# Squared-ReLU attention with a gated convolution network on one core: v's loads of batch 0 moved behind the planes' transfers, four banks for block 0's scores, and all low parts of the gated values on GpSimd

## The chip, the cores and the metric

The kernel runs on one core of one Trainium2 chip. The metric is the device time of one execution in microseconds (us), lower is better; the median of several runs is shown, and one further execution was taken with the hardware profiler. The engines are named as in the profile: PE (TensorE matmul; PEld its weight loads), DVE (VectorE), ACT (ScalarE), POOL (GpSimd), SP (SyncE, which here issues nearly all DMAs).

## The reference, cut to what matters

```python
# u, v: (4, 3136, 256), z: (4, 3136, 64)
scores = (1.0 / S) * np.matmul(z, z.transpose(0, 2, 1))      # S = 3136
attn = np.maximum(scores, 0.0) ** 2
x = u * np.matmul(attn, v)                                   # (4, 3136, 256)

h = np.maximum(x @ w_in, 0.0)                                # d_ff = 1024
conv_out[s] = sum(conv_w[k] * h_padded[s + k] for k in (0, 1, 2))   # per channel
gate = 1.0 / (1.0 + np.exp(-conv_out))
out = h * gate @ w_out                                       # (4, 3136, 256)
```

## The kernel before, in words

**Number format.** Most products are made from two 32-bit parts of each operand: a rounded "high" part (`ah`, `vh`, `gh`, `xh`, `zhh`) and the rest, "low" = value minus high (`al`, `vl`, `gl`, `xl`, `zll`). A product is three matmuls: high by low, high by high, low by high. Every value that goes into a matmul therefore costs one copy (`copy`, at line 125 of the profile for some) and one subtraction (`sub`, line 122 of the profile whoever runs it, on DVE or on POOL).

**Blocks and slots.** The 3136 rows of a batch are cut into 7 blocks of 448 columns (`QB = 7`), 28 blocks in all; q is the block's place in its batch. A block goes over the 25 tiles of 128 rows of its batch (`NJ = 25`). One tile of one block is a *slot*, numbered k = 25 * block + place, 700 in all. In slot k PE does the attention product of tile k (`attend`, lines 337 to 342: six matmuls) and then the scores of tile k + 4 (`scores`, lines 253 and 254: two matmuls into a PSUM bank with the tag `s`, of which there are two).

**From scores to attention.** For a computed tile: ACT takes the ReLU (`relu`, tile `t`, 3 buffers), DVE multiplies (`square`), ACT makes `ah`, DVE makes `al` (`split_lo`), which is the last reader of the scores' bank. The scores are symmetric, so later blocks of a batch don't compute every tile again: POOL takes the ReLU'd tile `t` apart into two 16-bit planes (`part`, tile `pl`, 3 buffers, line 270), SP writes them to DRAM (`spill`, `dq<-pl`, line 282), and a later block reads them back transposed (`fetch`, `tp<-dq`, line 290), joined by POOL (`join`, `tj<-tp`, line 296). Block q takes 0, 3, 7, 10, 14, 17 and 21 of its 25 tiles this way for q = 0 to 6. Block 0 of the kernel transposes nothing and spills most.

**v.** Two tiles of v at a time are loaded by SP (`load_v`, tile `vst`, 3 buffers, line 168), copied to `vh` by ACT (DVE for the first) and split to `vl` by POOL (`prep_v`). For batch 0 this runs inside block 0: tile j is prepared in slot j - 3.

**The network.** While block b + 1 does its attention, the network of block b runs in eight pieces f of 128 channels, begun in the slots `FS` = 2, 5, 8, 11, 15, 18, 21, 24 of block b + 1. With s the slot of a piece: `ffn_in` in slot s (six matmuls into one of two PSUM banks with the tag `ph`, lines 370 to 372); ReLU to `hb` on ACT and the first tap of the convolution back into the same bank in s + 1; POOL keeps two columns for the next block (`halo`, line 395), waiting for that ReLU; the other two taps on DVE (line 407) in s + 2; the sigmoid on ACT in s + 3; the gate product on DVE (line 421) in s + 4; the high part `gh` on ACT in s + 5; the low part `gl`; and `ffn_out` (lines 438 to 440) from slot s + 10 on.

In the blocks where `(blk + 1) % 7` is 3 to 6 ("V blocks" from here on, named by the block in whose slots the work runs: q = 3, 4, 5, 6) the gate product is written back in place into the `ph` bank, and the low part is made from that bank by DVE in slot s + 6. In the others ("G blocks", q = 0, 1, 2) the gate product goes to an SBUF tile `c`, and POOL makes the low part in slot s + 5. After the last slot, the last block's network runs alone (`last_block`), the tail.

**What sets the order.** Nothing is scheduled: every step is put in a list of its slot by `at(slot, class, ...)`, and the main loop empties the lists in the order of the classes PRE, MID, VEC, POST, PE0, PE1 around the fixed steps. Each engine, SP among them, runs its own instructions strictly in that order, and an instruction that waits holds up all behind it on its engine. Within a slot the POST class comes ahead of `fetch`, `join`, `part` and `spill`; PE1 comes after them, last of all.

Of the kernel before, what the change touches and what calls it, by code (L numbers as in the profile page):

```python
# [8 lines left out]
F32 = mybir.dt.float32  # L9
# [19 lines left out]
LA, LT, LS = 4, 3, 2  # L29
# [1 line left out]


FS = [2, 5, 8, 11, 15, 18, 21, 24]
RELU, TAP, ST1, ST2, SIG, GATE, GHI, GLO, OUT0, OUT1 = 1, 1, 2, 2, 3, 4, 5, 6, 10, 11
EVAC = 12
XS = 1

C_GATE, C_ST1, C_ST2, C_G, C_SIG, C_HI, C_LO = 0, 2, 2, 2, 3, 3, 2
C_TAP, C_XS, C_EV, C_V = 3, 3, 3, 5

QV = 3


WS = [0, 8, 11, 17, 15, 21, 27, 22, 29, 34, 36, 38, 40, 45, 48, 53]
# [14 lines left out]
def kernel(  # L59
# [15 lines left out]
    P = 128  # L75
    NB = 448
    QB = S // NB
    NJ = (S + P - 1) // P
# [11 lines left out]
    ps = ctx.enter_context(tc.tile_pool(name="ps", bufs=1, space=bass.MemoryType.PSUM))  # L90
# [14 lines left out]
    def at_slot(k):  # L105
        blk, i = divmod(k, NJ)
        return blk, *ent[blk % QB][i]
# [139 lines left out]
    def scores(k):  # L247
        blk, j, tr = at_slot(k)
        if tr:
            return  # L250
        s = ps.tile([P, 512], F32, tag="s", name="s", bufs=2)
        w = slice(j * P, (j + 1) * P)
        nc.tensor.matmul(s[:, :NB], lhsT=zhh[:, w], rhs=zq[blk], start=True, stop=False)  # L253
        nc.tensor.matmul(s[:, :NB], lhsT=zll[:, w], rhs=zq[blk], start=False, stop=True)  # L254
        sc[k] = s
# [108 lines left out]
    ph, hb, cc, gg, po = {}, {}, {}, {}, {}  # L364
# [30 lines left out]
            nc.gpsimd.tensor_copy(halo[:, f], t[:, NB : NB + 2])  # L395

    def ffn_tap(blk, f):
        e = width(blk)  # L400
        cc[blk, f] = c = ph.pop((blk, f))[:, :e]
        nc.scalar.mul(c, hb[blk, f][:, :e], cw[:, f, 0:1])  # L402
# [68 lines left out]
    V, A, G = nc.vector, nc.scalar, nc.gpsimd  # L471
# [4 lines left out]
    PRE, MID, VEC, POST, PE0, PE1 = range(6)  # L476

    def at(slot, cls, fn, *args):
        ev[slot][cls].append((fn, args))


    for q in range(2, QB):
        s = (7 * q) // 2 - LA - 2
# [1 line left out]
        at(s, POST, prep_z, q)  # L485
    at(-3, POST, prep_z, 1)
    for j in range(2, NJ, 2):
        at(max(j - 9, -LA), POST, load_v, 0, j)
        at(j - 3, C_V, prep_v, j, A)


    for b in range(1, B):
        k0 = (b * QB - 1) * NJ
        for q in range(QB):
            s = k0 - (QB - 2 - q) * NJ + (12 if q % 2 == 0 else 4)
            if q == QB - 2:
                s = k0 + 6
            elif q == QB - 1:
                s = k0 + NJ + 6
            at(s - 4, POST, load_z, b, q)  # L500
            at(s, POST, prep_z, q)
        last = {j: i for i, (j, _) in enumerate(ent[QB - 1])}
        for j in range(0, NJ, 2):
            s = k0 + max(last[j] + 2, last.get(j + 1, 0) + 2, V0 + V1 * j // NJ)
            at(s - 6, POST, load_v, b, j)
            at(s, C_V, prep_v, j, A)
    for blk in range(1, NBLK):
        at(blk * NJ - LA - 2, VEC, queries, blk)
# [2 lines left out]
    for i, (_, what, f) in enumerate(sorted(need)):  # L511
        s = WS[i]
# [8 lines left out]
    for blk in range(NBLK - 1):  # L521
        k0 = (blk + 1) * NJ
        at(k0, C_GATE, gate_x, blk, G)
        at(k0 + XS, C_XS, split_x, blk, (G, G))
        for f in range(FC):
            s = k0 + FS[f]
            at(s, POST, ffn_halo, blk, f)
            at(s, PE1, ffn_in, blk, f)
            at(s + RELU, C_TAP, ffn_relu, blk, f)
            at(s + TAP, C_TAP, ffn_tap, blk, f)  # L530
            at(s + ST1, C_ST1, ffn_conv, blk, f, 1)
            at(s + ST2, C_ST2, ffn_conv, blk, f, 2)
            at(s + SIG, C_SIG, ffn_sig, blk, f)
            lo = V if (blk + 1) % QB >= QV else G
            at(s + GATE, C_G, ffn_gate, blk, f, lo)
            at(s + GHI, C_HI, ffn_hi, blk, f, A)
            at(s + (GLO if lo is V else GHI), C_LO if lo is V else PE1, ffn_lo, blk, f, lo)
            at(s + OUT0, PE0, ffn_out, blk, f, 0)
            at(s + OUT1, PE0, ffn_out, blk, f, 1)
        at(s + EVAC, C_EV, evac, blk)  # L540
        at(s + EVAC + 2, POST, store, blk)
# [28 lines left out]
    with tc.manual_schedule():  # L570
# [12 lines left out]
        for k in range(-LA, max(ev) + 1):  # L583
            e = ev[k]
            run(e[PRE])
            if 0 <= k + LS < NS:
                split_hi(k + LS)
                split_lo(k + LS)
            run(e[MID])
            if 0 <= k + LT < NS:  # L590
                relu(k + LT)
                square(k + LT)
            run(e[VEC])
            run(e[POST])
            if 0 <= k + LD < NS:
                fetch(k + LD)
            if 0 <= k + LJ < NS:
                join(k + LJ)
            if 0 <= k + LP < NS:
                part(k + LP)  # L600
            if 0 <= k + LX < NS:
                spill(k + LX)
            run(e[PE0])
            if 0 <= k < NS:
                attend(k)
            if k + LA < NS:
                scores(k + LA)
            run(e[PE1])
# [41 lines left out]
```

## Time and profile before

| | us |
|---|---|
| median of 3 runs (1699.38 to 1700.0) | 1699.93 |
| the profiled execution | 1699.81 |
| its span, first to last instruction | 1697.7 |
| PE busy in the span | 1615.3 (95%) |
| ACT busy | 1277.1 (75%) |
| DVE busy | 1215.1 (72%) |
| POOL busy | 982.5 (58%) |

The mean granted TensorE clock was 0.992. How to read the views: busy time is the union of an engine's instructions. A matmul of 448 columns is listed at about 367 ns although a new one starts about every 203 ns, because they overlap; so the number of matmuls in a stretch says more about PE than its busy time. The view of waits gives, for each engine and line, who ended its idle time: the total in us, the number of waits, the longest. In the table of stretches each engine's busy us is followed by its number of instructions in brackets.

### The profile page before, as it was taken

What the parts mean: (1) busy time and instruction counts of PE and PEld (TensorE: products, weight loads), DVE (VectorE), ACT (ScalarE), POOL (GpSimd) and SP (SyncE); (2) the same over time, 40 slices, a digit from 0 to 9 for tenths busy, and PEclk for the clock granted to TensorE, in tenths of its full rate; (3) what the DMA queues carried; (4) which work ended last, traced back from release to release, by engine and by line L of the source; (5) the groups of instructions that cost most, each with busy time, mean ns of one, the idle gap of its engine ahead of it and who ended that gap; (6) DMA issues with size and microseconds to landing.
All of it is one profiled execution on the core that took longest, in us unless ns stands there. A gap on an engine that the chain in (4) does not pass through costs nothing.

```text
span 1697.7 us, 24837 instructions
## 1 busy us (share of the span) xinstructions
PE 1615.3 (95%) x7656; PEld 1433.9 (84%) x7656; DVE 1215.1 (72%) x2080; ACT 1277.1 (75%) x2562; POOL 982.5 (58%) x1345
## 2 busy tenths in 40 slices
PE   6689999999999999999999999999999999999998
PEld 5578888888889888888888988889889898888886
DVE  5788667776777767677767766777677776677766
ACT  5577777778777777777887777777877777777785
POOL 5767555556566654546575665555657566445551
PEclk9899999999999999999999999999999999999999
DMA  5543444456324434445543343454634334444540
GB/s 154 154 116 103 111 108 90 106 119 148 107 88 125 109 87 123 99 108 112 124 140 84 107 120 98 102 108 106 133 100 139 93 92 107 103 104 98 109 93 22
DMA packets 384485, 184.59 MB, mean 109 GB/s; under 512 B 275296, under 2 KB 383328, under 8 KB 384352
## 3 DMA queue, kind: packets, MB, share of 16 engines
q1 hardware_dynamic: 384208, 182.77, 43.5%
q8 instruction: 60, 0.98, 0.2%
q14 instruction: 73, 0.60, 0.1%
q10 hardware_dynamic: 144, 0.23, 0.0%
HBM read 36.59 MB, written 80.28 MB: 69 GB/s over the span
## 4 chain that ended last, share of the span: by engine, by line
PE 72%; DVE 13%; issue 6%; ACT 6%; POOL 1%; DMA 1%; SPq 0%; POOLq 0%; DVEq 0%; ACTq 0%
PE av L337 11%; PE av L338 11%; PE av L339 11%; PE ph L370 6%; PE ph L372 5%; PE ph L371 5%; PE s L253 5%; PE o L440 4%; PE o L438 4%; PE o L439 4%; PE s L254 4%; DVE al L122 3%; DVE s L309 3%; DVE ph L407 3%; ACT t L304 2%
## 5 line engine op out<-in xcount | busy, mean ns | idle before, releaser
L122 DVE TENSOR_TENSOR al<-s,ah 128x448 fp32r<-128x448 f32 x672 | 418.1, 622 | 369.1 <-ACT ah L316 198.4
L337 PE MATMUL av<-ah,vl 128*128 128x448 f32 x1344 | 496.0, 369 | 10.2 <-POOL vl L122 7.8
L338 PE MATMUL av<-ah,vh 128*128 128x448 f32 x1344 | 494.6, 368 | 0.0
L339 PE MATMUL av<-al,vh 128*128 128x448 f32 x1344 | 493.1, 367 | 0.0
L296 POOL COPY tj<-tp 128x896 uint16<-128x896 uint16 x288 | 348.4, 1214 | 1.9 <-DMA tp<-dq 1.5
L304 ACT ACTIVATE t<-s 128x448 f32<-128x448 f32 x412 | 225.4, 547 | 129.9 <-PE s L254 104.7
L407 DVE SCALAR_TENSOR_TENSOR ph<-hb,cw,ph 128x448 f32<-128x448 f32 (+1 forms) x448 | 306.8, 685 | 13.1 <-ACT ph L402 5.4
L309 DVE TENSOR_TENSOR s<-s,t 128x448 f32<-128x448 f32 x412 | 258.7, 628 | 78.2 <-ACT t L304 77.2
L270 POOL COPY pl<-t 128x896 uint16<-128x896 uint16 x312 | 290.7, 940 | 14.8 <-DMA dq<-pl 13.8
L395 POOL COPY halo<-hb 128x2 f32<-128x2 f32 x192 | 37.0, 192 | 451.1 <-ACT hb L393 450.7
L316 ACT CAST ah<-s 128x448 fp32r<-128x448 f32 x412 | 219.2, 532 | 98.0 <-DVE s L309 97.0
L337 PEld LDWEIGHTS av<-ah,vl 128*128 128x128 f32 x1344 | 254.6, 189 | 36.4 <-POOL vl L122 10.4
L339 PEld LDWEIGHTS av<-al,vh 128*128 128x128 f32 x1344 | 254.4, 189 | 21.3
L338 PEld LDWEIGHTS av<-ah,vh 128*128 128x128 f32 x1344 | 254.8, 190 | 20.4
L393 ACT ACTIVATE hb<-ph 128x448 f32<-128x448 f32 x224 | 122.6, 547 | 118.8 <-PE ph L372 117.2
L253 PE MATMUL s<-zq,zhh 128*128 128x448 f32 x412 | 163.6, 397 | 39.8 <-DVE al L122 31.0
L370 PE MATMUL ph<-xh,wih 128*128 128x448 f32 x448 | 171.9, 384 | 28.1 <-DVE gl L122 26.0
L314 ACT ACTIVATE ah<-tj 128x448 fp32r<-128x448 f32 x288 | 165.1, 573 | 0.0
L372 PE MATMUL ph<-xl,wih 128*128 128x448 f32 x448 | 164.8, 368 | 0.0
L438 PE MATMUL o<-gh,wol 128*128 128x448 f32 (+1 forms) x448 | 164.7, 368 | 0.0
L440 PE MATMUL o<-gl,woh 128*128 128x448 f32 (+1 forms) x448 | 164.1, 366 | 0.6 <-POOL gl L122 0.6
L371 PE MATMUL ph<-xh,wil 128*128 128x448 f32 x448 | 164.5, 367 | 0.0
(79 smaller groups left out, 2418.3 us busy)
## 6 DMA issues: line engine op xcount, KB each, us to landing
dq<-pl SPq DMA_DIRECT2D x252, 224.0 KB, 2.3
ut<-in_u_dram SPq DMA_DIRECT2D x28, 448.0 KB, 4.1
vst<-in_v_dram SPq DMA_DIRECT2D x48, 256.0 KB, 2.9
dq<-pl SPq DMA_DIRECT2D x84, 112.0 KB, 2.4
out_dram<-ob SPq DMA_DIRECT2D x20, 448.0 KB, 3.3
zt<-in_z_dram SPq DMA_DIRECT2D x28, 224.0 KB, 3.2
tp<-dq SPq DMA_TRANSPOSE x288, 3.3
wr<-in_moe_w_in_dram SPq DMA_DIRECT2D x8, 256.0 KB, 3.6
```

Of the source, the lines that this page charges most:

```text
L122: eng.tensor_tensor(out=out, in0=a, in1=b.bitcast(F32), op=ALU.subtract)
L270: nc.gpsimd.tensor_copy(pl[k], rl.pop(k).bitcast(U16).rearrange("p (n h) -> p h n", h=2))
L296: nc.gpsimd.tensor_copy(tj[k].bitcast(U16).rearrange("p (n h) -> p h n", h=2), t)
L304: nc.scalar.activation(rl[k], sc[k][:, :NB], AF.Relu, scale=SC1)
L309: nc.vector.tensor_tensor(out=s, in0=s, in1=rl[k], op=ALU.mult)
L337: nc.tensor.matmul(o, lhsT=vl[:, j, d], rhs=h, start=first, stop=False)
L338: nc.tensor.matmul(o, lhsT=vh[:, j, d], rhs=h, start=False, stop=False)
L339: nc.tensor.matmul(o, lhsT=vh[:, j, d], rhs=l, start=False, stop=False)
L370: nc.tensor.matmul(o, lhsT=wih[:, dc, w], rhs=xh[blk][:, dc], start=(dc == 0), stop=False)
L371: nc.tensor.matmul(o, lhsT=wil[:, dc, w], rhs=xh[blk][:, dc], start=False, stop=False)
L372: nc.tensor.matmul(o, lhsT=wih[:, dc, w], rhs=xl[blk][:, dc], start=False, stop=(dc == DC - 1))
L407: nc.vector.scalar_tensor_tensor(out=c, in0=hb[blk, f][:, k : e + k], scalar=cw[:, f, k : k + 1], in1=c, op0=ALU.mult, op1=ALU.add,)
```

## The change

Four edits. (1) `load_v` of batch 0 moves from class POST of slot j - 9 to class PE1 of slot j - 7, so behind that slot's `spill`. (2) `load_v` of the later batches moves from POST, six slots ahead of `prep_v`, to PE1, five slots ahead. (3) In block 0 (k < 25) the scores of odd k go to the two `ph` banks, those of even k stay in the two `s` banks. (4) The rule `QV` goes: in every block but the last the gate product goes to the SBUF tile `c`, and POOL makes the low part in class PE1 of slot s + 5. 128 gate products and 128 low parts (16 blocks of 8) are concerned.

```diff
-RELU, TAP, ST1, ST2, SIG, GATE, GHI, GLO, OUT0, OUT1 = 1, 1, 2, 2, 3, 4, 5, 6, 10, 11
+RELU, TAP, ST1, ST2, SIG, GATE, GHI, OUT0, OUT1 = 1, 1, 2, 2, 3, 4, 5, 10, 11
...
-QV = 3
...
-        s = ps.tile([P, 512], F32, tag="s", name="s", bufs=2)
+
+        tag = "ph" if k < NJ and k % 2 else "s"
+        s = ps.tile([P, 512], F32, tag=tag, name="s", bufs=2)
...
     for j in range(2, NJ, 2):
-        at(max(j - 9, -LA), POST, load_v, 0, j)
+        at(max(j - 7, -LA), PE1, load_v, 0, j)
         at(j - 3, C_V, prep_v, j, A)
...
-            at(s - 6, POST, load_v, b, j)
+            at(s - 5, PE1, load_v, b, j)
             at(s, C_V, prep_v, j, A)
...
-            lo = V if (blk + 1) % QB >= QV else G
-            at(s + GATE, C_G, ffn_gate, blk, f, lo)
+            at(s + GATE, C_G, ffn_gate, blk, f, G)
             at(s + GHI, C_HI, ffn_hi, blk, f, A)
-            at(s + (GLO if lo is V else GHI), C_LO if lo is V else PE1, ffn_lo, blk, f, lo)
+            at(s + GHI, PE1, ffn_lo, blk, f, G)
```

The line numbers shift by up to two: `sub` is line 120 after the change, the taps 406, the gate product 420, `load_v` 166.

What the edits move, as the order of instructions on the engines shows it. First SP in block 0, before, from the first planes' transfer on (`vst` is v's staging tile, `dq` the planes in DRAM; in square brackets the engines and queues whose progress the DMA waits for):

```order
L168 DMA vst<-in_v_dram 128x2x256 [waits DMAHW5_49,DMAHW3_49,Pool_49]
L282 DMA dq_205<-pl 64x2x448
L168 DMA vst<-in_v_dram 128x2x256 [waits DMAHW0_49,Pool_49]
L282 DMA dq_205<-pl 128x2x448 [waits DMAHW6_49]
L133 DMA zt<-in_z_dram 128x448 [waits DMAHW7_49]
L190 DMA wr<-in_moe_w_in_dram 128x2x128
L282 DMA dq_205<-pl 128x2x448 [waits DMAHW1_49]
L168 DMA vst<-in_v_dram 128x2x256 [waits DMAHW2_49,Pool_49]
```

The same place now:

```order
L166 DMA vst<-in_v_dram 128x2x256 [waits DMAHW5_49,Pool_49]
L282 DMA dq_203<-pl 64x2x448 [waits DMAHW3_49,Pool_49]
L282 DMA dq_203<-pl 128x2x448 [waits DMAHW4_49,Pool_49]
L166 DMA vst<-in_v_dram 128x2x256 [waits DMAHW7_49,Activation_49]
L131 DMA zt<-in_z_dram 128x448 [waits DMAHW6_49]
L188 DMA wr<-in_moe_w_in_dram 128x2x128
L282 DMA dq_203<-pl 128x2x448 [waits DMAHW0_49,Pool_49]
L282 DMA dq_203<-pl 128x2x448 [waits DMAHW1_49,Pool_49]
L166 DMA vst<-in_v_dram 128x2x256 [waits DMAHW2_49,Activation_49]
```

A load of v stood ahead of a plane's transfer and waited for POOL, while the transfer asked for nothing of POOL that the load had not waited for already; now each transfer waits for POOL itself, and the load stands behind it and waits for ACT.

PE in block 0, before, around slot 0 (`s` is the scores' bank):

```order
L339 MATMUL av_157<-al,vh 128x448
L253 MATMUL s<-zq,zhh 128x448 [waits DVE_49]
L254 MATMUL s<-zq,zll 128x448
L337 MATMUL av_156<-ah,vl 128x448 [waits Activation_49]
L338 MATMUL av_156<-ah,vh 128x448
L339 MATMUL av_156<-al,vh 128x448
```

and now:

```order
L339 MATMUL av_155<-al,vh 128x448
L253 MATMUL s<-zq,zhh 128x448
L254 MATMUL s<-zq,zll 128x448
L337 MATMUL av_154<-ah,vl 128x448 [waits Activation_49]
L338 MATMUL av_154<-ah,vh 128x448
L339 MATMUL av_154<-al,vh 128x448 [waits DVE_49]
```

The scores' wait for DVE is gone; the wait for `al` that DVE owes stands at the attention product that reads it.

DVE in the first V block (q = 3 of batch 0), before, over two pieces of the network (`s<-s,t` is the square, `al` the attention's low part, `ph<-hb,cw,ph` the taps, `ph<-ph,hb` the gate product, `gl` the low part):

```order
L309 TENSOR_TENSOR s<-s,t 128x448
L421 TENSOR_TENSOR ph<-ph,hb 128x448
L122 TENSOR_TENSOR al<-s,ah 128x448
L407 SCALAR_TENSOR_TENSOR ph<-hb,cw,ph 128x448 x2
L122 TENSOR_TENSOR al<-s,ah 128x448
L309 TENSOR_TENSOR s<-s,t 128x448
L122 TENSOR_TENSOR gl<-ph,gh 128x448
L122 TENSOR_TENSOR al<-s,ah 128x448
L421 TENSOR_TENSOR ph<-ph,hb 128x448
```

and now:

```order
L309 TENSOR_TENSOR s<-s,t 128x448
L420 TENSOR_TENSOR c<-ph,hb 128x448
L120 TENSOR_TENSOR al<-s,ah 128x448
L406 SCALAR_TENSOR_TENSOR ph<-hb,cw,ph 128x448 x2
L120 TENSOR_TENSOR al<-s,ah 128x448
L309 TENSOR_TENSOR s<-s,t 128x448
L120 TENSOR_TENSOR al<-s,ah 128x448
L420 TENSOR_TENSOR c<-ph,hb 128x448
```

The low part has left DVE, and the gate product writes `c`: from then on nothing reads the `ph` bank.

POOL at the same place now (`tj` a join, `pl` a part; before, the same rows stood there without the two `gl`):

```order
L296 COPY tj<-tp 128x2x448
L270 COPY pl<-t 128x896
L120 TENSOR_TENSOR gl<-c,gh 128x448
L386 COPY hb<-halo 128x2
L395 COPY halo<-hb 128x2
L270 COPY pl<-t 128x896
L296 COPY tj<-tp 128x2x448
L120 TENSOR_TENSOR gl<-c,gh 128x448
```

Each low part stands behind its slot's join and part, and ahead of the next piece's two `halo` copies.

More of the change, by code (lines that the diff above doesn't have):

```diff
@@ L33 @@
 FS = [2, 5, 8, 11, 15, 18, 21, 24]
-RELU, TAP, ST1, ST2, SIG, GATE, GHI, GLO, OUT0, OUT1 = 1, 1, 2, 2, 3, 4, 5, 6, 10, 11
+RELU, TAP, ST1, ST2, SIG, GATE, GHI, OUT0, OUT1 = 1, 1, 2, 2, 3, 4, 5, 10, 11
 EVAC = 12
 XS = 1
-C_GATE, C_ST1, C_ST2, C_G, C_SIG, C_HI, C_LO = 0, 2, 2, 2, 3, 3, 2
+C_GATE, C_ST1, C_ST2, C_G, C_SIG, C_HI = 0, 2, 2, 2, 3, 3
 C_TAP, C_XS, C_EV, C_V = 3, 3, 3, 5
-QV = 3
 WS = [0, 8, 11, 17, 15, 21, 27, 22, 29, 34, 36, 38, 40, 45, 48, 53]
```

## The prediction

> **What bounds the kernel now.** I read the table of stretches first, with one stretch for each of the first ten blocks (block b runs in row b + 1; columns: length, then busy us and instructions of PE, PEld, DVE, ACT, POOL, then the clock, the DMA share and GB/s), and one stretch of 50 us in which PE never idles.
>
> ```profile
> 11.47:84.06 72.59, 53.98 (x197) 41.97 (x196) 51.27 (x86) 40.65 (x88) 52.30 (x56) 0.88 0.52 152
> 84.06:150.40 66.34, 58.79 (x267) 51.49 (x266) 56.30 (x105) 49.33 (x108) 45.86 (x63) 0.95 0.44 120
> 150.40:210.90 60.50, 58.48 (x281) 52.20 (x282) 44.31 (x76) 45.77 (x93) 40.56 (x55) 1.00 0.38 100
> 210.90:271.20 60.30, 56.90 (x273) 50.59 (x272) 42.46 (x73) 44.25 (x89) 31.18 (x44) 1.00 0.44 106
> 271.20:329.50 58.30, 56.22 (x267) 49.25 (x266) 41.44 (x71) 43.83 (x89) 30.99 (x43) 1.00 0.47 103
> 329.50:384.00 54.50, 53.29 (x260) 48.16 (x260) 39.33 (x68) 43.70 (x89) 30.82 (x42) 1.00 0.50 107
> 384.00:439.70 55.70, 54.59 (x261) 48.20 (x260) 39.41 (x68) 46.06 (x94) 31.81 (x41) 1.00 0.54 122
> 439.70:501.60 61.90, 60.43 (x294) 54.27 (x293) 45.22 (x79) 48.41 (x97) 43.48 (x60) 1.00 0.40 120
> 501.60:560.50 58.90, 58.77 (x288) 53.36 (x286) 42.26 (x73) 43.75 (x88) 35.24 (x49) 1.00 0.40 112
> 560.50:619.90 59.40, 58.02 (x281) 52.25 (x282) 42.11 (x72) 44.97 (x90) 37.49 (x51) 1.00 0.39 102
> ...
> 1350.00:1400.00 50.00, 50.00 (x246) 45.54 (x245) 36.93 (x63) 36.93 (x75) 29.21 (x42) 1.00 0.39 101
> ```
>
> The last row gives PE's floor: 50.00 / 246 = 0.203 us a matmul. A block's length less its matmuls times 0.2033 is what PE loses there: 72.59 - 197 x 0.2033 = 32.5 us in block 0, 12.1 in block 1, 3.4 in block 2; in the V blocks 4.8, 4.0, 1.6 and 2.6 (13.1 together); in the next batch's G blocks 2.1, 0.3 and 2.3 (1.6 on the mean). So there are two places to gain: block 0, which is not bound by PE, and the four V blocks of each batch, where PE is the bound and waits. Who it waits for, from the view of waits over the whole span:
>
> ```profile
> PE s L253 <- DVE al L122: 31.0, 33, 2.6
> PE ph L370 <- DVE gl L122: 26.0, 35, 3.1
> PE av L337 <- POOL vl L122: 7.8, 7, 1.6
> ...
> PEld ph L370 <- DVE gl L122: 47.2, 59, 3.4
> ```
>
> The second row is the network's first matmul waiting for the `ph` bank that DVE's low part still reads. That work is exactly what edit 4 takes off the bank.
>
> **Block 0, edit 1.** The timeline shows one turn of the loop that holds it (start, us, what; in brackets the idle time before and who ended it):
>
> ```profile
> 27.78 0.94 POOL L270 COPY pl<-t 128x896 uint16<-128x896 uint16 x1 [1.92 <-DMA dq<-pl]
> ...
> 28.67 1.27 POOL L122 TENSOR_TENSOR vl<-vst,vh 128x512 fp32r<-128x512 f32 x1
> ...
> 29.97 0.37 SPq L168 DMA_DIRECT2D vst<-in_v_dram  x1
> ...
> 30.38 0.47 SPq L282 DMA_DIRECT2D dq<-pl  x1
> ...
> 31.08 0.93 POOL L270 COPY pl<-t 128x896 uint16<-128x896 uint16 x1 [1.14 <-DMA dq<-pl]
> ...
> 33.70 0.94 POOL L270 COPY pl<-t 128x896 uint16<-128x896 uint16 x1 [1.69 <-DMA dq<-pl]
> ```
>
> POOL finishes `vl` at 29.94; only then SP can issue the load of v (29.97), and only behind it the plane's transfer (30.38). POOL's part at 33.70 has stood idle 1.69 us for that transfer to land and free a `pl` buffer: POOL waits for SP, which waits for POOL. In totals, SP's and POOL's rows up to 84.06 us:
>
> ```profile
> SPq L168 <- POOL vl L122: 34.3, 9, 6.1
> ...
> POOL pl L270 <- DMA dq<-pl: 13.8, 8, 2.6
> ```
>
> In the new order a load comes behind the plane's transfer and reuses a buffer that was done with two slots before, so the transfers go out as soon as POOL has made them. The landing (30.38 to 33.6, 3.2 us) is then covered by the POOL work between a part and the third part after it: two parts of 0.94 and a `vl` of 1.27 at least, plus z and weights. I take the 13.8 us away, put 2 of it back for transfers that queue behind u's load, and keep POOL's busy time of 52.3. What is late next is DVE: 51.27 us busy. The largest share that DVE reaches anywhere is 56.30 / 66.34 = 85% in block 1; at that share block 0 lasts 51.27 / 0.85 = 60.3 us. So block 0 ends at about 61.5 us, **11 us less**. The ends: 4 us, if DVE takes most of it back (below), and 17, if all 13.8 go and the start of the ramp also shortens by the 3 us that the scores wait ahead of slot 0. The loads have time: tile j is asked for four slots, at 2.4 us each some 9 us, ahead of its copy, and the plane's transfer above took 3.2 to land.
>
> **Edit 3.** The scores' wait for `al` in block 0 and ahead of it is inside the first PE row above. With four banks it moves to the attention product, which needs the same `al` two slots later. While POOL and DVE set the pace that is a change of place, not of time: I cost it at nothing by itself. Its cover is the 32 us that PE idles in block 0 anyway; if that cover is gone (POOL and DVE faster than I think), it is worth up to 3 us more. The network loses nothing by it: the last odd tile, 23, is split in slot 21, and the first `ffn_in` comes in slot 27.
>
> **Edit 2.** One slot later (about 2.3 us) and behind that slot's transposes; PE's 7 waits for `vl` (7.8 us, above) all lie in block 0, so nothing waits for v in later batches. Nothing, with an end of 1 us lost for each of three batches.
>
> **Edit 4.** The operations that go and come, by form:
>
> ```profile
> L122 DVE TENSOR_TENSOR gl<-ph,gh 128x448 fp32r<-128x448 f32 x128 | 78.6, 614 | 0.0
> ...
> L122 POOL TENSOR_TENSOR gl<-c,gh 128x448 fp32r<-128x448 f32 x64 | 74.6, 1166 | 21.2 <-ACT gh L125 20.7
> ...
> L125 ACT CAST gh<-ph 128x448 fp32r<-128x448 f32 x128 | 67.8, 530 | 0.8 <-DVE ph L421 0.8
> ...
> L125 ACT CAST gh<-c 128x448 fp32r<-128x448 f32 x64 | 35.7, 557 | 0.0
> ```
>
> DVE loses 128 x 0.614 = 79 us, POOL gains 128 x 1.166 = 149 us, ACT gains 128 x 0.027 = 3.5 us, none of it on PE. What counts is the bank: it comes free with the gate product in slot s + 4 instead of the low part in slot s + 6, while `ffn_in` two pieces on wants it in slot s + 6 or later. Two slots of slack against waits of at most 3.1 us: I take all of them away. Of the row of 26.0 us in 35 waits, 3.65 lie in the tail (below), so 22.4 in 33 waits stand in the V blocks. A wait costs more than its idle time, since a matmul is shown 0.36 us long and the next could start after 0.203: 33 x 0.16 = 5.3, together 27.7. A second way: if each V block falls to the G blocks' mean loss, the gain is 13.1 - 4 x 1.6 = 6.7 a batch, 27 in four. The 24 waits that only the weight load shows (59 less 35) lie under 0.16 each, 2 us. **30 us**. The low end is 15: PE's own stops gave DVE time, and waits on `al` like the G blocks' can take their place. For the high end, these are the waits of the scores on `al` in the four V blocks of batch 0:
>
> ```profile
> PE s L253 <- DVE al L122: 1.9, 3, 0.7
> ...
> PEld s L253 <- DVE al L122: 5.8, 10, 1.1
> ```
>
> They stay: 1.9 + 3 x 0.16, and 0.16 for each of the other 7, is 3.5 a batch. The V blocks' whole loss less that, 4 x (13.1 - 3.5), is 38.
>
> What hides POOL's 149 us is its wait for the ReLU ahead of `halo`, once a piece, in the four V blocks of batch 0:
>
> ```profile
> POOL halo L395 <- ACT hb L393: 76.4, 28, 5.1
> ```
>
> 76.4 / 28 = 2.7 us a wait, against 1.17 for the low part that stands just ahead of it. POOL arrives later and waits less. By busy time the V blocks go from 31 to 31 + 8 x 1.166 = 40.5 of 55 to 60 us, less than the 43.48 of 61.90 that block 7 carries with a loss of 2.1. The closest place is the start of q = 6:
>
> ```profile
> 384.00:398.00 14.00, 14.00 (x67) 12.13 (x66) 8.97 (x15) 11.98 (x25) 10.32 (x14) 1.00 0.63 113
> ...
> 455.00:470.00 15.00, 15.00 (x76) 13.69 (x75) 9.39 (x17) 12.15 (x25) 12.10 (x18) 1.00 0.52 167
> ```
>
> 10.32 + 2 x 1.166 = 12.7 of 14 us there; 12.10 of 15 in the G row leaves PE without idle time. Behind the low part on POOL stand the next piece's `halo` copies and the joins; ACT waits for these, and DVE and PE for ACT.
>
> **The tail, also edit 4.** The last block's first `ffn_in` waits for the bank of piece 6 of block 26:
>
> ```profile
> 1667.85 0.74 PE L370 MATMUL ph<-xh,wih 128*128 128x448 f32 x1 [3.06 <-DVE gl L122]
> ...
> 1673.13 0.47 PE L370 MATMUL ph<-xh,wih 128*128 128x448 f32 x1 [0.59 <-DVE gl L122]
> ...
> 1662.90 0.63 DVE L421 TENSOR_TENSOR ph<-ph,hb 128x448 f32<-128x448 f32 x1
> 1664.79 1.16 DVE L122 TENSOR_TENSOR xl<-ut,xh 128x448 fp32r<-128x448 f32 x2 [1.26 <-ACT xh L360]
> ```
>
> The gate product of that piece ended at 1663.53; then the next thing needed is `xh` and the first `xl` (1665.4). PE can start at 1664.8 and waits some 0.6 for `xl`: 2.5 us sooner, and the second wait of 0.59 goes. DVE, busy with taps from there to the end, starts its first tap that much earlier. **3.5 us**, ends 1 and 4.5.
>
> **The sum**, against the profiled execution's 1699.81 (0.12 under the median; 2.1 us lie outside its span of 1697.7): 1699.8 - 11 - 30 - 3.5 = **1655.3**, so 1655. All low ends give 1699.8 - 4 - 15 - 1 = 1680, all high ends 1699.8 - 17 - 38 - 4.5 = 1640.
>
> **The rivals.**
>
> *R1, POOL falls behind: the other side.* If the moved low parts do not fit into POOL's waits, each pushes the next join, ACT's read of it, and PE by up to its whole 1.166 us: 128 x 1.166 = 149 lost against 44.5 gained. The point from which it decides: 44.5 / 128 = 0.35 us of delay for each. At 0.5 it ends at 1699.8 - 44.5 + 64 = 1719. For it: 12.7 of 14 us in the row above. Against it: 2.7 us of waiting for each 1.17, and the G blocks, which do the same with less slack. The Trainium skill's page "GPSIMD Engine Reference", section 4.1, says to leave elementwise adds of tiles to VectorE because GpSimd needs about twice as long. The trace agrees (1166 against 614 ns). If that doubled time all came to light, the whole would end at 1699.8 - 44.5 + 149 = 1804; by POOL's waits none of it does.
>
> *R2, DVE holds block 0.* DVE's weight preparation runs slower beside POOL:
>
> ```profile
> 33.16 0.28 DVE L207 TENSOR_SCALAR wm<-wr 128x256 uint32<-128x256 uint32 x1
> ...
> 44.69 1.21 DVE wm L207
> ```
>
> The same operation took 0.28 us at 33.16, where POOL stood idle, and 1.21 at 44.69, with POOL at work. Seven weight tiles of four such operations fall into block 0 (table `WS` up to 24). If POOL never pauses and each of the 28 takes 0.3 longer, DVE's 51.3 becomes 60, at 85% block 0 lasts 70: only 2 to 4 us come from it, and the result is 1699.8 - 3 - 30 - 3.5 = 1663. The same skill page's section 8 says that GpSimd shares its SBUF interfaces with VectorE and names two-input SBUF operations among those that contend. These two rows agree in direction; no row separates the causes.
>
> *R3, the next wait takes half of the V blocks.* The waits on `al` above lie in the same blocks. If PE, no longer held at `ffn_in`, reaches the scores before DVE has split, half of the 30 comes back: 1699.8 - 11 - 15 - 3.5 = 1670. Against it: DVE loses 8 x 0.614 = 4.9 us of some 41 in each V block.
>
> *R4, nothing moves*: the waits at the bank turn into equally long ones elsewhere and block 0 stays with DVE: 1699 to 1700.
>
> **How the numbers follow.** Forecast (1644 to 1661) 0.55; R2 0.17; R3 0.19; R4 0.03; R1 0.06. The first three are faster, 0.91 together; 0.2% (3.4 us) is about what a measurement of this kernel can tell from no change, so same 0.03, and R1 slower, 0.06. The range 1642 to 1678 holds the forecast, R2 and most of R3, within 2 us of the sums of all high and all low ends.
>
> **What would show it.** Edit 1: POOL's wait on `dq<-pl` under 4 us (13.8 now), SP's wait of v's loads on POOL gone, block 0 near 61 us. Edit 3: no wait of `s` on `al` ahead of block 1. Edit 4: no wait of `ph` on `gl`, POOL's wait at `halo` shorter by about 1.2 us a piece in the V blocks, their loss near 1.6 us each; the tail's first `ffn_in` some 3 us sooner after the last slot. It is wrong if ACT waits for `tj` or `ffn_out` for POOL's `gl` (R1), if block 0 stays above 67 us with DVE above 85% (R2), or if `s` on `al` grows by more than 10 us outside block 0 (R3).

## The result, and the profile after

The changed kernel takes **1644.96 us** (median of 4 runs, 1642.52 to 1647.3) against 1699.97 (4 runs, 1699.38 to 1701.4). The ratio is 0.9675, 95% interval 0.9658 to 0.9692: 55 us faster, where 44.5 were forecast, and inside the forecast's range (1642 to 1678). The profiled execution after took 1642.52 us with a span of 1640.5, so the two profiled executions that are compared below lie 57.3 us apart.

The table of stretches of after, same columns as before (block 0, block 1, the four V blocks of batch 0, and the first G block of batch 1):

```profile
9.24:70.32 61.08, 47.41 (x198) 39.57 (x196) 54.14 (x89) 41.34 (x91) 52.64 (x56) 0.92 0.63 183
70.32:135.20 64.88, 57.33 (x266) 50.32 (x266) 56.17 (x105) 49.08 (x107) 45.85 (x63) 0.97 0.46 124
...
195.80:252.00 56.20, 55.87 (x274) 50.95 (x273) 38.63 (x66) 43.86 (x89) 37.91 (x50) 1.00 0.53 110
252.00:307.90 55.90, 55.09 (x267) 49.62 (x266) 37.75 (x65) 44.29 (x89) 39.97 (x52) 1.00 0.50 107
307.90:360.50 52.60, 52.60 (x259) 48.37 (x258) 34.30 (x59) 43.17 (x88) 37.97 (x49) 1.00 0.51 110
360.50:415.50 55.00, 53.78 (x262) 48.64 (x262) 37.08 (x62) 46.91 (x95) 42.78 (x51) 1.00 0.58 129
415.50:476.20 60.70, 60.03 (x293) 54.34 (x292) 44.24 (x77) 48.15 (x97) 45.62 (x62) 1.00 0.41 122
```

Block 0 went from 72.6 to 61.1 us. By the prediction's reckoning (length less matmuls times 0.2033) the V blocks now lose 0.5, 1.6, nothing and 1.7, 3.8 together against 13.1. In the third of them PE is busy for its whole 52.60 us. POOL's busy time in a V block rose by 7 to 11 us, DVE's fell by 2 to 5.

The starts of all blocks in the two traces divide the difference as follows:

| place | us |
|---|---|
| ahead of slot 0 (11.47 to 9.24) | -2.2 |
| block 0 | -11.5 |
| block 1 | -1.5 |
| V blocks of four batches, and the G block behind each | about -39 |
| block 27 and the tail | -2.9 |

The view of waits of after, PE over the whole span (in us, times, longest), shows the wait of the network on `gl` gone but for one of 0.4 us in the tail, and the scores' wait on `al` down from 31.0 in 33. That fall lies in block 0, where the row was 9.6 in 8 and is 0.3 in 1; in the V blocks of batch 0 it was 1.9 in 3 and is 2.0 in 4.

```profile
PE s L253 <- DVE al L120: 19.5, 27, 2.3
PE av L337 <- POOL vl L120: 10.8, 8, 2.1
...
PE ph L370 <- DVE c L420: 0.8, 2, 0.6
...
PE ph L370 <- DVE gl L120: 0.4, 1, 0.4
```

The same view up to 75 us, SP's queue: `load_v` no longer stands in front of the planes, and what it waits for on POOL fell from 34.3 us in 9 to 3.9 in 2.

```profile
SPq L282 <- POOL pl L270: 27.5, 15, 4.0
SPq L166 <- POOL vl L120: 3.9, 2, 3.2
```

And in block 0 POOL's wait for a plane's transfer fell from 13.8 us in 8:

```profile
POOL pl L270 <- DMA dq<-pl: 0.9, 1, 0.9
```

In the four V blocks of batch 0, POOL's wait ahead of `halo` absorbed the moved work: 76.4 us in 28 became

```profile
POOL halo L395 <- ACT hb L393: 41.1, 23, 3.8
```

That is 35.3 us less for 32 low parts of 1.16 us (37.2 us).

### The profile page after: what moved, and what is told of

It is laid out like the page before. It is cut to its first block, busy times and chain, and to the rows that moved or that the text cites. A ratio compares the mean times of both kernels' runs of the same rounds, so it can differ in the third digit from the quotient of the medians.

```text
span 1640.5 us, 24863 instructions
## 1 busy us (share of the span) xinstructions
PE 1590.9 (97%) x7656; PEld 1434.7 (87%) x7656; DVE 1152.0 (70%) x1952; ACT 1276.3 (78%) x2562; POOL 1127.1 (69%) x1473
## 4 chain that ended last, share of the span: by engine, by line
PE 79%; DVE 8%; ACT 6%; issue 4%; POOL 2%; DMA 0%; POOLq 0%; DVEq 0%; SPq 0%; ACTq 0%
PE av L337 13%; PE av L338 13%; PE av L339 13%; PE s L253 6%; PE ph L372 5%; PE ph L370 5%; PE ph L371 5%; PE o L439 5%; PE o L437 5%; PE o L438 5%; PE s L254 5%; DVE al L120 3%; DVE ph L406 2%; DVE s L309 2%; ACT t L304 2%
## 5 line engine op out<-in xcount | busy, mean ns | idle before, releaser
L337 PE MATMUL av<-ah,vl 128*128 128x448 f32 x1344 | 494.3, 368 | 13.8 <-POOL vl L120 10.8
L406 DVE SCALAR_TENSOR_TENSOR ph<-hb,cw,ph 128x448 f32<-128x448 f32 (+1 forms) x448 | 306.8, 685 | 10.8 <-POOL gl L120 1.9
L309 DVE TENSOR_TENSOR s<-s,t 128x448 f32<-128x448 f32 x412 | 258.4, 627 | 59.4 <-ACT t L304 58.1
L120 POOL TENSOR_TENSOR gl<-c,gh 128x448 fp32r<-128x448 f32 (+1 forms) x220 | 256.2, 1165 | 62.4 <-ACT gh L123 60.4
L337 PEld LDWEIGHTS av<-ah,vl 128*128 128x128 f32 x1344 | 253.5, 189 | 40.3 <-POOL vl L120 13.8
L370 PE MATMUL ph<-xh,wih 128*128 128x448 f32 x448 | 164.4, 367 | 1.3 <-DVE c L420 0.8
```

Of the source, the lines that this page charges most:

```text
L120: eng.tensor_tensor(out=out, in0=a, in1=b.bitcast(F32), op=ALU.subtract)
L309: nc.vector.tensor_tensor(out=s, in0=s, in1=rl[k], op=ALU.mult)
L337: nc.tensor.matmul(o, lhsT=vl[:, j, d], rhs=h, start=first, stop=False)
L370: nc.tensor.matmul(o, lhsT=wih[:, dc, w], rhs=xh[blk][:, dc], start=(dc == 0), stop=False)
L406: nc.vector.scalar_tensor_tensor(out=c, in0=hb[blk, f][:, k : e + k], scalar=cw[:, f, k : k + 1], in1=c, op0=ALU.mult, op1=ALU.add,)
```

## The experiments

Four kernels ran first, on one chip (before there: 1699.92 us): edits 4, 1 and 3 alone, and a variant of edit 4.

**Edit 4 alone.** The gate product writes `c` and POOL makes every low part; the rest is the kernel before.

```diff
-            lo = V if (blk + 1) % QB >= QV else G
+            lo = G
```

> Edit 4 alone; block 0 and all loads as before. Bank theory: all of the gain outside block 0 comes with it, 39 us in the V blocks and 3 in the tail as the two profiles are compared: about 1657 us, PE's wait of ph on gl gone in the V blocks, block 0 still 72 to 73 us long. Rival, the parts help each other (a faster block 0 is needed for the rest): 1665 us or more.

Measured 1657.23 us (1656.51 to 1657.69), ratio 0.9748 (0.9734 to 0.9763): 42.7 us. The V blocks of batch 0 are 56.2, 55.8, 52.6 and 54.8 us long, within 0.2 of the changed kernel's, and block 0 is still 71.65. Edit 4 is worth more than the 33.5 given to it and its tail.

**Edit 1 alone.**

```diff
-        at(max(j - 9, -LA), POST, load_v, 0, j)
+        at(max(j - 7, -LA), PE1, load_v, 0, j)
```

> Edit 1 alone: v's loads of batch 0 behind the planes' transfers, two banks for the scores, all else as before. Theory that SP's order made block 0's loop: POOL's wait on dq<-pl falls from 13.8 to under 3 us, block 0 from 72.6 to 61 to 64 us, 1687 to 1690 us in all. Rival, the banks made the gain: block 0 stays above 70, 1697 to 1700 us.

Measured 1689.38 us (1688.62 to 1689.86), ratio 0.9937 (0.9923 to 0.9952): 10.5 us. The stretch of block 0, then PE's largest wait and POOL's wait for the planes from 9 to 84 us:

```profile
11.32:73.10 61.78, 46.52 (x198) 36.18 (x196) 55.10 (x87) 40.23 (x89) 52.34 (x56) 1.00 0.59 175
```

```profile
PE s L253 <- DVE al L122: 16.2, 16, 1.8
...
POOL pl L270 <- DMA dq<-pl: 1.0, 1, 1.0
```

POOL's wait for the planes, 13.8 us before, is gone but for 1.0. Block 0 has nearly its final length with two banks for the scores, and PE still waits 16.2 us for `al`: that wait does not set the pace.

**Edit 3 alone.**

```diff
-        s = ps.tile([P, 512], F32, tag="s", name="s", bufs=2)
+        tag = "ph" if k < NJ and k % 2 else "s"
+        s = ps.tile([P, 512], F32, tag=tag, name="s", bufs=2)
```

> Edit 3 alone: four banks for block 0's scores, loads and network as before. SP's order theory: the waits of s on al go, but POOL still waits for dq<-pl by 10 us or more, and only the start ahead of slot 0 gets 2 us shorter: 1696 to 1699 us. Rival, the banks made the gain: block 0 at 61 to 64 us, 1688 us.

Measured 1698.41 us (10 runs, 1696.39 to 1699.62), ratio 0.9989 (0.9979 to 0.9998): 1.5 us. Slot 0 starts 2.2 us earlier, at 9.27, but block 0 is 73.95 long. Its waits from 9 to 84 us:

```profile
PE av L339 <- POOL vl L122: 18.3, 10, 2.7
...
POOL pl L272 <- DMA dq<-pl: 14.4, 8, 3.2
```

The wait on `al` became one on `vl`, and POOL still waits 14.4 us for the planes. The three together make 42.7 + 10.5 + 1.5 = 54.7, and all four edits 55.0: the edits add up.

**Bank or engine? The product in `c`, the low part still on DVE.** Edit 4 frees the `ph` bank and relieves DVE. Here only the bank is freed: the V blocks' gate product goes to `c`, and DVE makes the low part from it in slot s + 6, as before.

```diff
-        if lo is nc.gpsimd:
+        if blk < NBLK - 1 or lo is nc.gpsimd:
```

> Half of edit 4 on the kernel before: in the V blocks the gate product goes to the SBUF tile c, so the bank comes free in slot s + 4, but DVE still makes the low part (from c) in slot s + 6. Bank theory: nearly all of edit 4's gain is here, V blocks at 53 to 56.5 us, 1657 to 1664 us. Rival, the gain is DVE's 79 us less work: V blocks stay within 1 us of 60.3, 58.3, 54.5 and 55.7, 1690 us or more.

Measured 1664.01 us (1663.78 to 1664.84), ratio 0.979 (0.9773 to 0.9806): 35.9 of the 42.7, at the edge of what was expected. The first two V blocks of batch 0 (the second is above the 53 to 56.5 named), then three rows of PE's waits over the span:

```profile
211.30:267.70 56.40, 56.07 (x274) 50.84 (x273) 42.34 (x72) 44.00 (x89) 31.58 (x44) 1.00 0.50 111
267.70:324.80 57.10, 55.20 (x267) 49.71 (x267) 43.86 (x73) 44.13 (x89) 32.03 (x44) 1.00 0.49 107
```

```profile
PE s L253 <- DVE al L122: 34.7, 39, 2.6
PE av L337 <- POOL vl L122: 7.9, 7, 2.0
PE av L337 <- DVE ut L348: 5.2, 5, 2.4
```

Freeing the bank alone takes the V blocks most of the way. The 6.8 us that remain go with DVE's load: with 79 us of low parts still on it, the scores wait 34.7 us for `al`, 30.7 with edit 4 alone, and a block's first attention product 5.2 us in 5 for `ut`, which DVE makes from the previous block's result (2.4 in 1 with edit 4 alone).

**The other half: DVE relieved, the bank still held.** The changed kernel, with a one-column copy by DVE on the `ph` bank where the low part used to stand, in slot s + 6 of the V blocks.

```diff
+        bank[blk, f] = c
...
+    def hold(blk, f):
+        c = bank.pop((blk, f))
+        nc.vector.tensor_copy(c[:, 0:1], c[:, 0:1])
...
+            if (blk + 1) % QB >= 3:
+                at(s + 6, 2, hold, blk, f)
```

> The changed kernel, with one thing put back: in the V blocks a copy of one column on DVE in slot s + 6 still reads the ph bank, so the bank is held as long as before, while GpSimd makes the low part and DVE is relieved of it. The copy's result isn't used. Bank theory: the V blocks go back to near 60, 58, 54.5 and 55.5 us, 1675 to 1684 us. Rival, DVE's relief made the gain: 1645 to 1650 us.

Measured 1658.64 us (1657.67 to 1659.57), ratio 0.9766 (0.975 to 0.9783), before on that chip 1698.72. That is about 14 us more than the changed kernel (15 more than the two variants that ran beside it at 1643.41 and 1643.8, below), between the two theories, and neither expectation holds. The network waits for the bank again, but less often and less long than the 26.0 in 35 of before:

```profile
PE ph L370 <- DVE ph L427: 10.4, 18, 2.7
```

The longest of these waits, 2.7 us, is in the tail. And the bank was not held as long as before: in the V blocks the one-column copy ends 4.29 us on the mean after the gate product, the low part of before ended 4.89 us after it. The copy takes 0.16 us, the low part took 0.61. So this kernel relieves DVE and shortens the hold at once, and by its time alone the two can't be told apart.

An account of PE can. For each matmul, take the time since the start of the one before it, less 0.2033 us. Here these losses are summed over the V blocks of all batches and the block behind each four (q = 0), which hold 5082 matmuls in every run; length and losses are in us:

| kernel | length | lost at `ffn_in` (`ph`) | at the scores (`s`) | elsewhere |
|---|---|---|---|---|
| before | 1095.3 | 40.8 | 21.1 | 0.2 |
| changed | 1055.6 | -0.2 | 22.5 | 0.1 |
| edit 4 alone | 1055.5 | -0.3 | 22.5 | 0.1 |
| product in `c`, low part on DVE | 1061.8 | -0.3 | 24.3 | 4.6 |
| bank held by the copy | 1069.0 | 16.6 | 19.4 | -0.3 |

What edit 4 gains in these blocks, 39.7 us, is the loss at the bank, all of it; the scores lose no less than before. With the bank free but the low part still on DVE, 6.4 us turn up at the scores and at the attention products that wait for `ut`. With the copy, what stays lost is again lost at the bank, and of the 26.3 us that this kernel gains on before in these blocks 24.2 are gained there, with the bank let go 0.6 us sooner.

**Twice the work on POOL.** Each of the 128 moved low parts is made twice, so POOL has 149 us more.

```diff
-    def ffn_lo(blk, f, eng):
+    def ffn_lo(blk, f, eng, n=1):
...
+        for _ in range(n):
+            sub(eng, g[1][:, :e], c, g[0][:, :e])
...
-            at(s + GHI, PE1, ffn_lo, blk, f, G)
+            at(s + GHI, PE1, ffn_lo, blk, f, G, 2 if (blk + 1) % QB >= 3 else 1)
```

> The changed kernel with each of the 128 moved low parts made twice on GpSimd, 149 us more work for POOL in the V blocks, some 8 x 1.17 = 9.3 us a block. Theory that POOL's waits for the ReLU hide it: these waits are 41.1 us in 23 in the four V blocks of batch 0, 1.8 us each, so most of a second 1.17 is hidden too: 1645 to 1660 us. Rival R1, POOL has no room: each is exposed, 1645 + 149 = 1794 us; anything above 1700 speaks for it.

Measured 1664.74 us (1664.16 to 1665.32), ratio 0.98: 19.8 us more than the changed kernel, some 5 above what was expected, 13% of the added work. It falls mostly on q = 6, 55.0 us long in batch 0 after the change:

```profile
363.50:423.50 60.00, 55.58 (x261) 49.67 (x260) 36.90 (x62) 47.15 (x95) 52.92 (x61) 0.97 0.52 118
```

POOL is busy 52.92 of 60.00 us there. In the other V blocks of batch 0 the doubling cost 0 to 0.5 us. This is where R1 would begin; one low part stays below it.

**Does POOL hold block 0?** In block 0 of after, POOL runs from 14.5 to 66.4 us with pauses of 1.5 us in all. Seven of its 22 parts go to ACT:

```diff
-        nc.gpsimd.tensor_copy(pl[k], rl.pop(k).bitcast(U16).rearrange("p (n h) -> p h n", h=2))
+        eng = nc.scalar if k < NJ and k % 3 == 1 else nc.gpsimd
+        copy(eng, pl[k], rl.pop(k).bitcast(U16).rearrange("p (n h) -> p h n", h=2))
```

> The changed kernel with every third part of block 0 (7 of 22, 0.94 us each on POOL) copied by ACT instead. If POOL's work alone now sets block 0's pace, 6.6 us less on POOL makes block 0 5 to 6 us shorter: 55 to 56 us, 1639 us in all. If DVE binds (54.1 us busy of 61.1), block 0 gets at most 2 us shorter: 1643 to 1645 us.

Measured 1643.41 us (1642.77 to 1645.74), ratio 0.9677 (0.9663 to 0.9692):

```profile
8.96:70.80 61.84, 50.17 (x197) 40.65 (x196) 53.07 (x89) 46.48 (x98) 45.95 (x49) 0.89 0.60 182
```

POOL lost 6.7 us, ACT got 5.1 more, and the block gained nothing. POOL is nearly always busy there, and its work alone is still not the bound.

**Edit 2 undone.**

```diff
-            at(s - 5, PE1, load_v, b, j)
+            at(s - 6, POST, load_v, b, j)
```

> The changed kernel with edit 2 undone: the later batches' loads of v again in class POST six slots ahead. The loads land 8 us or more ahead of their copy either way, so nothing moves: 1643 to 1647 us, blocks 6 and 7 of each batch within 0.3 us. Rival, the loads' place on SP feeds the transposes: blocks of q = 6 and q = 0 change by over 1 us each, 3 us or more in all.

Measured 1643.8 us (1641.45 to 1645.13), ratio 0.9676 (0.9661 to 0.969): no difference from the changed kernel.

**Does DVE hold block 0?** The squares of the odd slots below 50 go from DVE to ACT.

```diff
+SQ = 50
...
-            nc.vector.tensor_tensor(out=s, in0=s, in1=rl[k], op=ALU.mult)
+            if k < SQ and k % 2:
+                nc.scalar.activation(s, rl[k], AF.Square, scale=SC1**-0.5)
+            else:
+                nc.vector.tensor_tensor(out=s, in0=s, in1=rl[k], op=ALU.mult)
```

> The changed kernel with the square of every odd slot of blocks 0 and 1 made by ACT instead of DVE (12 in block 0, 7.5 us off DVE, 6.6 us onto ACT). Seven parts off POOL left block 0 as long as it was, so the theory is now that DVE and its hand-overs with ACT set block 0's pace (54 us busy of 61): block 0 falls to 55 to 58 us and block 1 from 65 to 62, 1636 to 1641 us. Rival, POOL still binds, since it never paused for long between 14.5 and 66.4 us: block 0 stays within 1 us of 61, at most block 1 gains.

Measured 1644.03 us (1642.9 to 1644.58), ratio 0.9682 (0.9667 to 0.9696), before on that chip 1698.07. Blocks 0 and 1:

```profile
8.90:69.20 60.30, 45.42 (x197) 37.89 (x196) 50.44 (x76) 47.16 (x103) 51.71 (x55) 0.96 0.62 185
69.20:136.30 67.10, 59.33 (x266) 52.15 (x264) 52.06 (x96) 53.96 (x117) 46.11 (x64) 0.94 0.44 120
```

DVE has 3.7 us less in block 0, half of the 7.5 that were meant: its squares fell from 16.2 to 8.1 us between 9 and 70 us, but the four steps of weight preparation took 23.7 us instead of 20.7. Block 0 is 0.8 us shorter, and block 1 gives that back with 2.2 more. The 55 to 58 us of the DVE theory did not come, but the relief was smaller than planned.

**Both reliefs together**, the two diffs above in one kernel.

> Both reliefs in block 0: seven parts from POOL to ACT and the odd slots' squares from DVE to ACT (blocks 0 and 1). If DVE alone binds, it ends with the kernel that moves the squares alone, within 1 us. If POOL comes next right behind DVE, block 0 gets 3 us or more shorter than there: 1633 to 1637 us. If ACT is now the bound (41 + 6.6 + 6.6 us of work in block 0), it is no better than the squares alone or worse.

Measured 1641.59 us (1641.26 to 1643.94), ratio 0.9668 (0.9651 to 0.9684); the changed kernel on the same chip, below, has 1644.3 and 0.9687 (0.9672 to 0.9701). The intervals overlap, so a gain is not shown.

```profile
8.96:68.40 59.44, 47.94 (x197) 39.22 (x196) 48.55 (x76) 52.36 (x110) 45.31 (x48) 0.91 0.63 189
```

**The squares on ACT, and q = 6 without POOL's low part** (there DVE makes it from `c`).

```diff
-            at(s + GHI, PE1, ffn_lo, blk, f, G)
+            if (blk + 1) % QB == QB - 1:
+                at(s + 6, 2, ffn_lo, blk, f, V)
+            else:
+                at(s + GHI, PE1, ffn_lo, blk, f, G)
```

> The squares of odd slots of blocks 0 and 1 on ACT, and in the blocks q = 6, where POOL has least room (42.8 us busy of 55.0), the low part again on DVE but from the SBUF tile c, in slot s + 6. With the low part on DVE from c these blocks lasted 54.2 us against 54.9 with it on POOL: 2 to 3 us less than with the squares alone. Rival: DVE's work there costs the block after it what it gains, 0 to 1 us.

Measured 1644.69 us (1643.95 to 1645.19), ratio 0.9686 (0.9672 to 0.9701): the 2 to 3 us did not come, q = 6 stayed at 54.9 and 55.1.

**The changed kernel once more**, unaltered.

> The changed kernel unaltered, beside the three others on the same chip: 1643 to 1647 us.

Measured 1644.3 us (1643.97 to 1646.5), ratio 0.9687 (0.9672 to 0.9701). Its block 0:

```profile
9.00:71.60 62.60, 48.58 (x198) 39.73 (x196) 56.08 (x89) 41.57 (x92) 52.52 (x56) 0.92 0.60 179
```

The same kernel's block 0 took 61.1 and 62.6 us in two profiles, and 61.8 to 62.3 in the three variants above that leave blocks 0 and 1 as they are. The 61.8 with the parts moved is no change. With the squares moved block 0 took 60.3, 59.4 and 60.4, a little less than all of these, but block 1 took it back: blocks 0 and 1 together last 126.6 to 127.4 us there, 125.9 to 128.3 without. None of the variants is shown to beat the changed kernel.

## Why the prediction came out as it did

*Block 0, edit 1: right.* Forecast 11 less and 61.5 us long; it became 61.1, and alone the edit gave 10.5. POOL's wait for the planes fell to 0.9 us, where under 4 was named. A wait of SP on POOL for v's loads stayed, 3.9 us, where none was named; it now stands behind the transfers. The reason given for the new length, DVE at its 85%, was not borne out: DVE is at 54.14 / 61.08 = 89%, so that figure was no ceiling, and 3.7 us less DVE work hardly shortened the block. What sets its pace of 60 us is open. Taking 7 us of POOL away didn't move it; taking 4 of DVE or both away moved it by 1 to 2 us, which block 1 took back. A chain of hand-overs between engines that each work in order would look like this, but no run isolated it.

*Edit 3: a little, not nothing.* It was costed at nothing, with "up to 3 us more" at the end of the range. Slot 0 started 2.2 us earlier, with block 0 fast enough to keep that; alone the edit gave 1.5, of which block 0 gave part back. As forecast, the scores' wait on `al` left block 0, but for one of 0.3 us at its end; the attention product waits more for `vl` instead (10.8 us in 8, before 7.8 in 7).

*Edit 2: nothing,* as taken.

*Edit 4 in the V blocks: right mechanism, mis-sized term,* 30 us against about 39. Two steps failed. The first is the price of one wait, its idle time plus 0.16. PE's timeline of before at a wait in q = 3 shows what else a wait costs:

```profile
262.34 0.47 PE L370 MATMUL ph<-xh,wih 128*128 128x448 f32 x1 [0.77 <-DVE gl L122]
262.64 0.36 PE L371 MATMUL ph<-xh,wil 128*128 128x448 f32 x1
```

The matmul behind the waiting one starts 0.30 later, not 0.203: another 0.1 us. Counted from start to start, with that second matmul, the forecast's 33 waits in the blocks cost 31.1 us, where it took 27.7. The waits that only the weight load shows it took as 24 of under 0.16 each, 2 us; 14 of them moved the matmul by 0.08 us or more, and these cost 4.3. And 15 more at the same matmul, which the profile puts down to no wait for `gl` (12 to "issue", 3 to ACT), cost 4.2 and were put at nothing; after the change they are gone too. Together these are 39.6 us. In q = 3 of batch 0 the price of a wait closes the account by itself. The view of waits of before, PE in that block alone:

```profile
PE ph L370 <- DVE gl L122: 3.2, 4, 1.2
```

3.2 + 4 x (0.16 + 0.1) = 4.2 us; the block became 4.1 shorter with one matmul more. The second step is the comparison with the G blocks' mean loss of 1.6: the V blocks lost 0.95 on the mean after the change, and the G block behind each four gained 1.1 too, so that cross-check agreed with 30 by an error of its own. The waits on `al` stayed in the V blocks, as the forecast's high end of 38 had it, and that end was nearly the result.

"What counts is the bank" is borne out: freeing it alone gave 35.9 of the 42.7, and by PE's account its loss was the whole gain in these blocks. What the forecast left out is that DVE's relief keeps another 6.8 us from turning up elsewhere. The forecast's cover held: POOL's wait at `halo` fell by 35.3 / 32 = 1.1 us a piece (1.2 were named), and POOL's 149 us cost nothing visible.

*The tail: 2.3 us of the 3.5.* The last block's first `ffn_in` came 3.0 us sooner after the last attention product, as said. But the step "DVE starts its first tap that much earlier" failed. ACT's timeline of before, then those of ACT, POOL and DVE after (the last attention product started at 1661.38 before and at 1606.60 after):

```profile
1668.59 0.53 ACT L125 CAST gh<-ph 128x448 fp32r<-128x448 f32 x1 [0.76 <-DVE ph L421]
1670.50 0.55 ACT L393 ACTIVATE hb<-ph 128x448 f32<-128x448 f32 x1 [1.37 <-PE ph L372]
```

```profile
1613.80 0.57 ACT L123 CAST gh<-c 128x448 fp32r<-128x448 f32 x1 [0.75 <-DVE c L420]
1614.28 0.54 ACT L393 ACTIVATE hb<-ph 128x448 f32<-128x448 f32 x1
1614.90 0.64 ACT L401 ACTIVATE ph<-hb,cw 128x450 f32<-128x450 f32 x1
```

```profile
1612.12 0.19 POOL L386 COPY hb<-halo 128x2 f32<-128x2 f32 x1
...
1614.45 1.15 POOL L120 TENSOR_TENSOR gl<-c,gh 128x448 fp32r<-128x448 f32 x1 [1.94 <-ACT gh L123]
```

```profile
1615.65 0.69 DVE L406 SCALAR_TENSOR_TENSOR ph<-hb,cw,ph 128x450 f32<-128x450 f32 x1 [1.93 <-POOL gl L120]
```

Before, ACT's first ReLU of the last block waited for PE, so an earlier `ffn_in` could help it. After, PE is done in time, but on ACT the ReLU stands behind the previous block's last `gh`, and that comes 7.2 us after the last attention product in both. So ReLU, ACT's tap and DVE's first tap follow only 1.4 us sooner: DVE's starts 9.05 us after the last attention product instead of 10.48 (1671.86 before). The view names POOL's low part as what ended DVE's wait, but that one ended by chance at the same time: the edge columns that the tap needs were written at 1612.12, ahead of the low part, and ACT's tap had read them at 1614.90. From the second piece's ReLU on (1615.48, before 1672.58) the gain is 2.3 us.

*The rivals.* R1 (1719) did not come: 0.35 us for each low part would have used up the gain, and even doubling POOL's work cost 19.8 / 128 = 0.15. The Trainium skill's page "GPSIMD Engine Reference", section 4.1, would have kept the operation on VectorE; its factor of two agrees with 1164 against 614 ns here, but what it would make of the time does not follow while POOL waits. R2 failed with block 0 at 61.1: DVE's 28 weight operations took 20.1 us in block 0 before and 20.7 after, not 0.3 longer each. Its two rows did not hold in general, either: the same operation took 0.28 us at 55.84 and 62.35 too, with POOL at work. R3 failed: the scores' waits on `al` neither grew nor fell with edit 4 alone (30.7 us in 37, before 31.0 in 33). R4 failed.

## What to carry to other kernels

A wait on the bounding engine costs more than its idle time: measure it from start to start, the next instruction too (here 0.26 us on top of each). Where several waits hang together, sum the losses of the bounding engine by what it was about to do, over blocks of equal work: that told the bank's share from DVE's here, where the run made for it did not. A shared bank should be given up by the earliest short reader; where the reader behind it moves to a slower engine, look for that engine's wait once a turn, which is what pays for the move. A releaser named in a view can be the last of several semaphores: check whether what the instruction needs was there before. An in-order queue should not have a load that waits for a buffer ahead of a transfer on which that buffer's owner waits: 10.5 us here for two numbers in one line.

## What was not expected of the hardware

After an idle time of 2.15 us the matmul's spacing nearly doubles for three microseconds. PE's timeline of after in block 0:

```profile
35.22 0.47 PE L337 MATMUL av<-ah,vl 128*128 128x448 f32 x1 [1.73 <-POOL vl L120]
...
40.87 0.47 PE L337 MATMUL av<-ah,vl 128*128 128x448 f32 x1 [2.15 <-POOL vl L120]
...
42.22 0.58 PE L339 MATMUL av<-al,vh 128*128 128x448 f32 x1
42.59 0.58 PE L253 MATMUL s<-zq,zhh 128*128 128x448 f32 x1
...
45.17 0.36 PE L339 MATMUL av<-al,vh 128*128 128x448 f32 x1
45.37 0.36 PE L253 MATMUL s<-zq,zhh 128*128 128x448 f32 x1
```

From 41.85 to 44.83 matmuls start every 0.37 us, then again every 0.20. The wait of 1.73 had no such stretch behind it, the one of 2.15 had. But the length of a single wait doesn't decide it: in the same trace PE waited 2.43 us up to 135.18, and no slow stretch followed. The table of stretches shows the difference (PE's busy time comes second, the granted clock third from the end):

```profile
38.29:41.70 3.41, 1.26 (x7) 0.84 (x6) 3.41 (x5) 2.22 (x5) 3.41 (x4) 1.00 0.92 285
41.70:45.11 3.41, 3.41 (x11) 3.05 (x10) 2.81 (x6) 1.05 (x3) 3.04 (x4) 0.50 0.73 222
...
130.45:133.86 3.41, 2.30 (x12) 1.78 (x10) 3.37 (x7) 2.06 (x6) 2.18 (x3) 1.00 0.88 214
133.86:137.27 3.41, 2.09 (x10) 1.96 (x11) 2.79 (x6) 2.89 (x7) 2.13 (x3) 1.00 0.02 5
```

The clock is halved from 41.70, 62.18 and 99.72 on, which lie 6 and 17 times 3.413 us after the first. On that grid the idle 2.15 us fall into one stretch, and the 2.43 are split over two. In the traces of all runs, from 8 us to 1630 us, each such stretch at full clock with more than 1.9 us of idle time was followed by half clock, and none with less than 1.5. With more but shorter waits (edit 1 alone, none over 1.8 us on `al`) the granted clock of block 0 was 1.00. The Trainium skill's page "TensorE: Matmul & The Clock Gate", Part 1, gives half clock after one idle window of some 3.4 us; the length of the slow stretch here agrees with such a window, but no idle time of PE around it is that long. The mean clock of the whole span is 0.995, so over the span this is worth some 0.005 x 1640 = 8 us of PE's time.
